# First-layer matmuls for two token blocks at once, and another order of two integer steps on GpSimd

## The chip, the cores and the metric

The kernel runs on one core of one Trainium2 chip. The metric is device time in microseconds: median of several runs. The engines are TensorE (PE, with its weight loads shown as PEld), VectorE (DVE), ScalarE (ACT), GpSimd (POOL) and SyncE (SP), which issues the DMAs.

## The reference, cut to what matters

```python
# attention, q, k, v: (8, 8, 576, 64), top_k = 32
scores = scale * np.matmul(q, k.transpose(0, 1, 3, 2))
kth = np.partition(scores, -top_k, axis=-1)[..., -top_k:-top_k + 1]
scores = np.where(scores >= kth, scores, -1000000000.0)
attn = np.exp(scores - np.max(scores, axis=-1, keepdims=True))
attn = attn / (np.sum(attn, axis=-1, keepdims=True) + 1e-09)
out = np.matmul(attn, v)
# the heads side by side: x is (4608, 512); w_in (512, 2048), w_out (2048, 512)
h = x @ w_in
g = h * (1.0 / (1.0 + np.exp(-1.702 * h)))
return g @ w_out
```

## The kernel before, in words

The attention is cut into 144 slots, 18 for each of the 8 batches. A slot is 128 rows of queries for two heads. Each batch has four full tiles of 128 tokens and a tail of 64; the tails of two batches make one block together. For a slot, TensorE computes the scores (L283), ScalarE copies them to SBUF (L295, tile `sc`), and VectorE finds the 32nd largest score of each row. From slot 12 on it does so from halves: `pair_up` takes the larger of each two scores (`greater`, VectorE, L324) and GpSimd finds the smaller (`lesser`) on the bits as integers: the sum of both (L327), less the larger (L328). Rounds of MAX8 and MATCH_REPLACE8 (L345, L348) search both halves; `pair_up` of the next slot stands in the midst of them. From the results come `cut` and, on GpSimd, `low` (L378, in slots up to 11 `cut` and `low` at L389 and L390). ScalarE masks (Prelu, L398) and takes the exponentials (L401), splits the words (L471), and a DMA through DRAM turns them. In slots up to 12, TensorE turns them instead, with a diagonal `by` (GpSimd, L414). TensorE multiplies by the values (L539, tile `o`), ScalarE copies the result (`x`, L924), and GpSimd's `x_of` scales it into the block's `xT` (L553).

When all eight heads of a block's 128 tokens are done, `finish_x` puts the block on the list `ready`. The feed-forward layers are fed to TensorE in small calls among the attention's matmuls: `hidden` does the first layer for four of a block's sixteen chunks of the hidden width (16 matmuls of 128 columns, L587, into a PSUM tile `ph`), `tanh` takes the tanh on ScalarE (L604) and copies the rest (`h`, L607), `gate` multiplies on GpSimd (L616, L617; at the end of the kernel on VectorE, L619), `project` does the second layer for the same chunks (four matmuls of 512 columns, L635, into `po`), and `leave` copies a finished `po` to `ob` (L641) and sends it out (L643). There are 36 blocks, so 144 calls of `hidden` and of `project`.

The order is written by hand and each engine works through its own queue in that order. `slot` issues slots 0 to 12, `two_slots` two slots at a time after that, with two calls of `hidden` and of `project`, and `last_slot` what is left at the end. PSUM has a pool `ps_t` with two buffers (for `o`, for every second `ph`, for transposes), `ps_h` with one (for the other `ph`) and `ps_p` with one (for `po`). The blocks' inputs `xT` come from a pool of four buffers for full tiles and one for tails, which `by` shares.

Of the kernel before, what the change touches and what calls it, by code (L numbers as in the profile page):

```python
# [9 lines left out]
ALU = mybir.AluOpType  # L10
ENG = mybir.EngineType
F32 = mybir.dt.float32
U32 = mybir.dt.uint32
I32 = mybir.dt.int32
# [4 lines left out]
P = 128  # L19
# [3 lines left out]
RAISE = 2.0**8  # L23
# [7 lines left out]
def kernel(  # L31
# [27 lines left out]
    nc = tc.nc  # L59

    B, H, S, D = q.shape
    C = H * D
    DFF = moe_w_in.shape[1]
    NP = H // 2
    NF = S // P
    FULL = NF * P
    TAIL = S - FULL
    HALF = S // 2
    CC = C // P
    FC = DFF // P  # L70
    G = 4
    NG = FC // G
# [17 lines left out]
    const = ctx.enter_context(tc.tile_pool(name="const", bufs=1))  # L90
    pool = lambda name, bufs, **kw: ctx.enter_context(tc.tile_pool(name=name, bufs=bufs, **kw))
# [6 lines left out]
    lefts = pool("lefts", 2)  # L98
    small = pool("small", 4)
    ptp = pool("ptp", 2)  # L100
    xtp = pool("xtp", 4)
    xtt = pool("xtt", 1)
    thp = pool("thp", 5)
    apart = pool("apart", 4, space=DRAM)
    apart_qk = pool("apart_qk", 2, space=DRAM)
# [1 line left out]
    ps_t = pool("ps_t", 2, space=PSUM)  # L107
    ps_h = pool("ps_h", 1, space=PSUM)
    ps_p = pool("ps_p", 1, space=PSUM)
# [4 lines left out]
    wout = const.tile([P, FC, C], F32, name="wout")  # L114
# [156 lines left out]
    st = [{} for _ in slots]  # L271
# [45 lines left out]
    greater, lesser = {}, {}  # L317

    def pair_up(n):

        sc = st[n]["sc"]
        a, b = sc[:, :, 0:HALF], sc[:, :, HALF:S]
        greater[n] = lefts.tile([P, 2, HALF], F32, name="greater", tag="left")
        nc.vector.tensor_tensor(out=greater[n][:], in0=a, in1=b, op=ALU.max)  # L324
        lesser[n] = raws.tile([P, 2, HALF], F32, name="lesser", tag="raw")
        whole = lesser[n][:].bitcast(I32)
        nc.gpsimd.tensor_tensor(out=whole, in0=a.bitcast(I32), in1=b.bitcast(I32), op=ALU.add)  # L327
        nc.gpsimd.tensor_tensor(out=whole, in0=whole, in1=greater[n][:].bitcast(I32), op=ALU.subtract)  # L328

    def topk_of_pairs(n):  # L330

# [74 lines left out]
    def divide(n):  # L406

        some = small.tile([P, 2], F32, name="some", tag="sums")
        nc.vector.tensor_scalar_add(some[:], st[n]["den"], 1e-9)
        rden = small.tile([P, 2], F32, name="rden", tag="inverse")  # L410
        nc.vector.reciprocal(rden[:], some[:])
        by = st[n]["by"] = xtt.tile([P, 2, P], F32, name="by", tag="xT_t")
        for i in range(2):
            nc.gpsimd.tensor_scalar(by[:, i, :], ident[:], rden[:, i : i + 1], 1.0, op0=ALU.mult, op1=ALU.mult)  # L414

# [62 lines left out]
        pt = st[n]["pt"] = ptp.tile([P, 2 * NF + 1, P], F32, name="pt")  # L478
        nc.sync.dma_start_transpose(out=pt[:].bitcast(U16), in_=rows[:].rearrange("q h k -> (q h) k"))

    xts = {}

    def x_at(b, t, hp):

        if t < NF:
            if (b, t) not in xts:
                xts[b, t] = xtp.tile([P, CC, P], F32, name="xT")
            return xts[b, t][:, hp, :]
        if b // 2 not in xts:
            xts[b // 2] = xtt.tile([P, CC, P], F32, name="xT_t")  # L490
        return xts[b // 2][:, hp, b % 2 * TAIL : (b % 2 + 1) * TAIL]

    def values(n, put_off=None):

# [19 lines left out]
        def bring():  # L514
            for o, hp in outs:
                to = x_at(b, t, hp)
                nc.scalar.copy(out=to, in_=o[:, 0 : to.shape[-1]])
            finish_x(n)
# [29 lines left out]
    def x_of(m, o, by):  # L548

        b, t, hps = slots[m]  # L550
        for p in range(2 if t == NF else 1):
            cols = slice(p * TAIL, (p + 1) * TAIL) if t == NF else slice(0, P)
            nc.gpsimd.tensor_tensor(out=x_at(b, t, hps[p]), in0=o[:, cols], in1=by[:, cols], op=ALU.mult)  # L553
        finish_x(m)

    def finish_x(m):

        b, t, hps = slots[m]
        if hps[-1] < NP - 1:
            return  # L560
        if t == NF:
            if b % 2:
                first = [(b - 1 + i) * S + FULL for i in range(2)]
                rows = [(slice(i * TAIL, (i + 1) * TAIL), out[x : x + TAIL, :]) for i, x in enumerate(first)]
                xT = xts.pop(b // 2)
                ready.append(([xT[:, c, :] for c in range(CC)], [rows]))
            return
        lines = out[b * S : b * S + FULL, :].rearrange("(p t) c -> p t c", t=NF)
        xT = xts.pop((b, t))
        ready.append(([xT[:, c, :] for c in range(CC)], [[(slice(0, P), lines[:, t, :])]]))  # L570

    ready = []
    hidden_at = {"f": 0}
    to_gate, gated, to_project = [], [], []
    pos = []

    def hidden(into=None):
        if not ready:
            return
        xT, rows = ready[0]  # L580
        tiles = len(rows)
        f0 = hidden_at["f"]
        fs = range(f0, f0 + G // tiles)
        ph = (into or ps_h).tile([P, G * P], F32, name="ph", tag="tp" if into else "ph")
        for i, f in enumerate(fs):
            for c in range(CC):
                nc.tensor.matmul(  # L587
                    ph[:, i * tiles * P : (i + 1) * tiles * P],
                    lhsT=win[:, c, f * P : (f + 1) * P],
                    rhs=xT[c],  # L590
                    start=(c == 0),
                    stop=(c == CC - 1),
                )
        to_gate.append((ph, fs, rows))
        hidden_at["f"] = fs.stop % FC
        if fs.stop == FC:
            ready.pop(0)

    def tanh(aside):

        if to_gate:
            ph, g, rows = to_gate.pop(0)
            th = thp.tile([P, G * P], F32, name="th")
            nc.scalar.activation(th[:], ph[:], AF.Tanh, scale=0.851 / RAISE)  # L604
            if aside:
                h = raws.tile([P, G * P], F32, name="h", tag="raw")
                nc.scalar.copy(out=h[:], in_=ph[:])  # L607
                ph = h
            gated.append((th, ph, g, rows))

    def gate(aside):
        if not gated:
            return
        th, h, g, rows = gated.pop(0)
        if aside:
            nc.gpsimd.tensor_scalar(th[:], th[:], 1.0, 1.0, op0=ALU.add, op1=ALU.mult)  # L616
            nc.gpsimd.tensor_tensor(out=th[:], in0=th[:], in1=h[:], op=ALU.mult)  # L617
        else:
            nc.vector.scalar_tensor_tensor(  # L619
                out=th[:], in0=th[:], scalar=1.0, in1=h[:], op0=ALU.add, op1=ALU.mult  # L620
            )
        to_project.append((th, g, rows))

    def project(put_off_leaving=False):

        gT, fs, rows = to_project.pop(0)
        if fs.start == 0:
            pos[:] = [
                home.tile([P, C], F32, name="po", tag=tag) for home, tag in ((ps_p, "po"), (ps_h, "ph"))[: len(rows)]
            ]  # L630
        blocks = iter(range(G))
        for f in fs:
            for po in pos:
                i = next(blocks)
                nc.tensor.matmul(  # L635
                    po[:], lhsT=gT[:, i * P : (i + 1) * P], rhs=wout[:, f, :], start=(f == 0), stop=(f == FC - 1)
                )
        if fs.stop == FC:
            def leave(po, to_rows):
                ob = thp.tile([P, C], F32, name="ob", tag="th")  # L640
                nc.scalar.mul(out=ob[:], in_=po[:], mul=0.5 / RAISE**2)  # L641
                for on, to in to_rows:
                    nc.sync.dma_start(to, ob[on, :])  # L643

            leaving.extend(lambda po=po, to=to: leave(po, to) for po, to in zip(pos, rows))
            if not put_off_leaving:
                leave_all()

    leaving = []

    def leave_all():
        while leaving:
            leaving.pop(0)()
# [16 lines left out]
    for n in by_slot:  # L670
        first = sum(map(len, list(by_slot.values())[:n]))
# [20 lines left out]
    finished = []  # L692
# [3 lines left out]

    def may_project(waiting):

        return len(to_project) > waiting and len(finished) >= NG * CC + to_project[0][1].stop

    def both_heads(to, src, t):

# [67 lines left out]
    def slot(n):  # L770
# [25 lines left out]
        for i, op in enumerate(topk_of_pairs(n) if n >= PAIRED else topk(n)):  # L796
            op()
            if i == 2:
                for _ in range(min(3 if n >= TURNS else 6, len(unfinished))):
                    finish_one()  # L800
            if i == 5:
                if n > 0:
                    divide(n - 1)
                while unfinished:
                    finish_one()
            if i == 10:
                gate(False)
# [30 lines left out]
        if n > PROJECTS and may_project(2):  # L838
            project()
        if idle:  # L840
            stay_warm(8)
        hidden()

    def last_slot():

        tanh(False)
        hidden(ps_t if hidden_at["f"] % (2 * G) else None)
        gate(False)
        if may_project(0):
            project()  # L850
# [133 lines left out]
```

## Time and profile before

| | |
|---|---|
| median of 3 runs | 1480.8 us (1480.79 to 1482.15) |
| the profiled execution's own time | 1482.51 us |
| its span | 1480.7 us |
| mean granted TensorE clock | 0.989 |
| first layer, L587 | 4608 records of 128 columns |
| second layer, L635 | 1152 records of 512 columns |
| `greater`, L324 | x132, mean 1165 ns, median 759 ns |

How to read it: busy time is the union of an engine's instructions. A matmul's record lasts longer than the array is taken by it, since matmuls overlap; what a matmul costs is seen from start to start. Each matmul of the program shows as two records. In the timeline's lines the columns are start, duration, engine, line, operation, output from input, count; brackets give the idle time before and what ended it.

### The profile page before, as it was taken

What the parts mean: (1) busy time and instruction counts of PE and PEld (TensorE: products, weight loads), DVE (VectorE), ACT (ScalarE), POOL (GpSimd) and SP (SyncE); (2) the same over time, 40 slices, a digit from 0 to 9 for tenths busy, and PEclk for the clock granted to TensorE, in tenths of its full rate; (3) what the DMA queues carried; (4) which work ended last, traced back from release to release, by engine and by line L of the source; (5) the groups of instructions that cost most, each with busy time, mean ns of one, the idle gap of its engine ahead of it and who ended that gap; (6) DMA issues with size and microseconds to landing.
All of it is one profiled execution on the core that took longest, in us unless ns stands there. A gap on an engine that the chain in (4) does not pass through costs nothing.

```text
span 1480.7 us, 31436 instructions
## 1 busy us (share of the span) xinstructions
PE 1442.7 (97%) x10784; PEld 1056.0 (71%) x10784; DVE 1382.9 (93%) x4541; ACT 1177.6 (80%) x1865; POOL 859.2 (58%) x1119
## 2 busy tenths in 40 slices
PE   7789899999999999999999999999999999999998
PEld 5667656777777777777777777777777777777776
DVE  7999989999999999999999999999999999999920
ACT  7998688878788887888878797888878798777730
POOL 3777545566655665666656556665565566665610
PEclk8899999999999999999999999999999999999999
DMA  8451256767667676776678686675767766545430
GB/s 245 135 156 51 72 159 180 202 172 179 173 181 201 159 196 179 178 189 178 170 180 200 168 193 171 183 195 163 179 175 203 174 187 184 140 131 132 127 87 15
DMA packets 516321, 242.20 MB, mean 164 GB/s; under 512 B 452672, under 2 KB 490560, under 8 KB 516160
## 3 DMA queue, kind: packets, MB, share of 16 engines
q1 hardware_dynamic: 515728, 239.89, 61.6%
q8 instruction: 85, 1.39, 0.4%
q14 instruction: 76, 0.62, 0.1%
q10 hardware_dynamic: 432, 0.30, 0.1%
HBM read 45.09 MB, written 102.24 MB: 99 GB/s over the span
## 4 chain that ended last, share of the span: by engine, by line
PE 88%; DVE 10%; ACT 2%; issue 0%; POOL 0%; POOLq 0%; ACTq 0%; DVEq 0%
PE ph L587 34%; PE po L635 32%; PE o L539 10%; PE s_ps L283 10%; DVE top L305 4%; DVE left L308 3%; PE o L528 1%; DVE top L345 1%; PE tp L449 1%; DVE wout L153 0%; DVE left L348 0%; PE none L170 0%; DVE greater L324 0%; ACT pr L401 0%; DVE win L153 0%
## 5 line engine op out<-in xcount | busy, mean ns | idle before, releaser
L635 PE MATMUL po<-wout,th 128*128 128x512 f32 x1152 | 518.6, 593 | 1.1 <-ACT ob L641 1.1
L587 PEld LDWEIGHTS ph<-xT,win 128*128 128x128 f32 x4096 | 472.1, 192 | 53.8 <-issue 52.2
L587 PE MATMUL ph<-xT,win 128*128 128x128 f32 x4096 | 484.4, 277 | 0.0
L635 PEld LDWEIGHTS po<-wout,th 128*128 128x128 f32 x1152 | 208.0, 190 | 211.0 <-issue 208.5
L345 DVE MAX8 top<-left 128x8 f32<-128x288 f32 x792 | 325.2, 445 | 0.0
L471 ACT COPY sc<-pr 128x2304 uint16<-128x2304 uint16 x132 | 278.8, 2112 | 4.2
L295 ACT ACTIVATE sc<-s_ps 128x576 f32<-128x576 f32 x288 | 170.9, 646 | 130.2 <-PE s_ps L283 130.2
L328 POOL TENSOR_TENSOR lesser<-lesser,greater 128x576 int32<-128x576 int32 x132 | 186.2, 1411 | 126.5 <-DVE greater L324 126.3
L348 DVE MATCH_REPLACE8 left<-top,left 128x288 f32<-128x288 f32 x528 | 229.6, 442 | 0.0
L401 ACT ACTIVATE pr<-sc,low 128x576 f32<-128x576 f32 x288 | 220.7, 772 | 0.0
L398 ACT ACTIVATE sc<-sc,cut 128x576 f32<-128x576 f32 x288 | 207.2, 772 | 12.4 <-DVE cut L357 5.8
L345 DVE MAX8 top<-lesser 128x8 f32<-128x288 f32 x528 | 213.5, 444 | 0.0
L327 POOL TENSOR_TENSOR lesser<-sc 128x576 int32<-128x576 int32 x132 | 187.0, 1417 | 2.4 <-ACT sc L295 2.4
L283 PE MATMUL s_ps<-qk_t 64*128 64x288 f32 (+1 forms) x1280 | 183.2, 433 | 0.3 <-ACT qk_t L219 0.3
L617 POOL TENSOR_TENSOR th<-th,h 128x512 f32<-128x512 f32 x128 | 163.7, 1279 | 10.7
L378 POOL TENSOR_SCALAR low<-cut,top 128x1 f32<-128x1 f32 x264 | 65.7, 265 | 175.6 <-DVE cut L357 174.1
L324 DVE TENSOR_TENSOR greater<-sc 128x576 f32<-128x576 f32 x132 | 153.8, 1165 | 11.7 <-ACT sc L295 5.5
L539 PE MATMUL o<-pt,v_l 128*64 128x128 f32 (+1 forms) x2368 | 144.4, 265 | 0.0
L539 PEld LDWEIGHTS o<-pt,v_l 128*64 128x64 f32 x2368 | 120.6, 138 | 25.7 <-issue 22.9
L604 ACT ACTIVATE th<-ph 128x512 f32<-128x512 f32 x144 | 85.9, 596 | 54.9 <-PE ph L587 48.3
L283 PEld LDWEIGHTS s_ps<-qk_t 64*128 64x128 f32 (+1 forms) x1280 | 99.4, 178 | 41.0 <-issue 23.1
L348 DVE MATCH_REPLACE8 left<-top,greater 128x288 f32<-128x288 f32 x264 | 114.7, 442 | 0.0
(86 smaller groups left out, 1535.7 us busy)
## 6 DMA issues: line engine op xcount, KB each, us to landing
rows<-sc SPq DMA_DIRECT2D x132, 576.0 KB, 3.2
qk_rows<-halves SPq DMA_DIRECT2D x48, 256.0 KB, 2.8
qk_l<-in_q_dram SPq DMA_DIRECT2D x64, 128.0 KB, 2.9
raw<-in_moe_w_in_dram SPq DMA_DIRECT2D x16, 512.0 KB, 4.9
v_l<-in_v_dram SPq DMA_DIRECT2D x32, 256.0 KB, 3.1
raw<-in_moe_w_out_dram SPq DMA_DIRECT2D x16, 512.0 KB, 3.5
out_dram<-ob SPq DMA_DIRECT2D x32, 256.0 KB, 2.9
qk_l<-in_k_dram SPq DMA_DIRECT2D x62, 128.0 KB, 2.9
```

What stands on the lines that cost most here:

```text
L283: nc.tensor.matmul(ps[i][rows, c, 0:HALF], lhsT=qT[b, hps[p]][on, cols], rhs=kT[b, hps[p]][on, FIRST[i] + c * HALF : FIRST[i] + (c + 1) * ...
L295: nc.scalar.mul(out=to, in_=ps[i][:, :, 0:HALF], mul=SCALE)
L327: nc.gpsimd.tensor_tensor(out=whole, in0=a.bitcast(I32), in1=b.bitcast(I32), op=ALU.add)
L328: nc.gpsimd.tensor_tensor(out=whole, in0=whole, in1=greater[n][:].bitcast(I32), op=ALU.subtract)
L345: nc.vector.max(found(r, i, True), src[:, i, :])
L348: nc.vector.match_replace(to[:, i, :], found(r, i), src[:, i, :], LOWEST)
L398: nc.scalar.activation(sc[:, i, :], sc[:, i, :], AF.Prelu, bias=cut[:, i : i + 1], alpha=HUGE)
L401: nc.scalar.activation(pr[:, i * S : (i + 1) * S], sc[:, i, :], AF.Exp, bias=low[:, i : i + 1], accum_out=den[:, i : i + 1],)
L471: nc.scalar.copy(out=halves, in_=pr[:].bitcast(U16).rearrange("p (k h) -> p h k", h=2))
L539: nc.tensor.matmul(o[j * D : (j + 1) * D, cols], lhsT=main[:, j, c, :] if c < NF else tail[:, j, :], rhs=pt[:, MAIN[j] + c if c < NF else ...
L587: nc.tensor.matmul(ph[:, i * tiles * P : (i + 1) * tiles * P], lhsT=win[:, c, f * P : (f + 1) * P], rhs=xT[c], start=(c == 0), stop=(c == ...
L635: nc.tensor.matmul(po[:], lhsT=gT[:, i * P : (i + 1) * P], rhs=wout[:, f, :], start=(f == 0), stop=(f == FC - 1))
```

## The change

`hidden` looks at the first two blocks on `ready`. If there are two, one call does two chunks for both (8 matmuls, each with 256 columns: 128 of one block and 128 of the other), else four chunks of the one as before. The chunks are taken from those that the first block still lacks, so a block's second half is computed together with its successor, which does its first half, by number, later and alone or with the block after it. All `xT` lie in one tile of five places, so that two blocks' columns can be read with one stride; `by` uses a part of place 4. Two blocks' `po` can be open at once; the second sits in `ps_h`, and `hidden` then uses `ps_t`. In `pair_up` GpSimd subtracts the larger first and adds the other score after that.

```diff
-    xtp = pool("xtp", 4)
-    xtt = pool("xtt", 1)
+    xs = const.tile([P, 5, CC, P], F32, name="xT")
...
-        nc.gpsimd.tensor_tensor(out=whole, in0=a.bitcast(I32), in1=b.bitcast(I32), op=ALU.add)
-        nc.gpsimd.tensor_tensor(out=whole, in0=whole, in1=greater[n][:].bitcast(I32), op=ALU.subtract)
+        nc.gpsimd.tensor_tensor(out=whole, in0=a.bitcast(I32), in1=greater[n][:].bitcast(I32), op=ALU.subtract)
+        nc.gpsimd.tensor_tensor(out=whole, in0=whole, in1=b.bitcast(I32), op=ALU.add)
...
-        by = st[n]["by"] = xtt.tile([P, 2, P], F32, name="by", tag="xT_t")
+        by = st[n]["by"] = xs[:, 4, 0:2, :]
...
+    class Block:
+        def __init__(self, place, rows):
+            self.place, self.rows = place, rows
+            self.left = list(range(FC))
+            self.done = 0
...
     def hidden(into=None):
         if not ready:
             return
-        xT, rows = ready[0]
-        tiles = len(rows)
-        f0 = hidden_at["f"]
-        fs = range(f0, f0 + G // tiles)
+        blocks = ready[:2]
+        many = len(blocks)
+        fs = blocks[0].left[: G // many]
+        first, step = min(x.place for x in blocks), abs(blocks[0].place - blocks[-1].place) or 1
+        blocks = sorted(blocks, key=lambda x: x.place)
+        into = ps_t if many > 1 or pos["other"] else into
         ph = (into or ps_h).tile([P, G * P], F32, name="ph", tag="tp" if into else "ph")
         for i, f in enumerate(fs):
             for c in range(CC):
                 nc.tensor.matmul(
-                    ph[:, i * tiles * P : (i + 1) * tiles * P],
+                    ph[:, i * many * P : (i + 1) * many * P],
                     lhsT=win[:, c, f * P : (f + 1) * P],
-                    rhs=xT[c],
+                    rhs=xs[:, first : first + step * (many - 1) + 1 : step, c, :],
...
+        for x in blocks:
+            x.left = [f for f in x.left if f not in fs]
+        if many > 1:
+            pos["other"] = True
+        while ready and not ready[0].left:
+            free.append(ready.pop(0).place)
+            if len(ready) < 1 or len(ready[0].left) == FC:
+                pos["other"] = False
...
     def project(put_off_leaving=False):
-        gT, fs, rows = to_project.pop(0)
...
+        gT, fs, blocks = to_project.pop(0)
+        for x in blocks:
+            if not x.done:
+                home = "ps_h" if "ps_p" in in_use else "ps_p"
+                in_use.append(home)
+                x.home = home
+                pool_of, tag = (ps_h, "ph") if home == "ps_h" else (ps_p, "po")
+                x.po = pool_of.tile([P, C], F32, name="po", tag=tag)
+        i = 0
         for f in fs:
-            for po in pos:
-                i = next(blocks)
+            for x in blocks:
                 nc.tensor.matmul(
-                    po[:], lhsT=gT[:, i * P : (i + 1) * P], rhs=wout[:, f, :], start=(f == 0), stop=(f == FC - 1)
+                    x.po[:], lhsT=gT[:, i * P : (i + 1) * P], rhs=wout[:, f, :], start=(x.done == 0), stop=(x.done == FC - 1)
                 )
...
+        for x in blocks:
+            if x.done == FC:
+                in_use.remove(x.home)
+                leaving.append(lambda x=x: leave(x))
...
     def last_slot():
 
         tanh(False)
-        hidden(ps_t if hidden_at["f"] % (2 * G) else None)
+        last["turn"] += 1
+        hidden(ps_t if last["turn"] % 2 else None)
```

More of the change, by code (lines that the diff above doesn't have):

```diff
@@ L479, in turn_by_dma @@
         nc.sync.dma_start_transpose(out=pt[:].bitcast(U16), in_=rows[:].rearrange("q h k -> (q h) k"))
-    xts = {}
+    places = {}
+    free = [4, 0, 1, 2, 3]
     def x_at(b, t, hp):
[L485 to L491, printed above, removed]
+        name = (b, t) if t < NF else b // 2
+        if name not in places:
+            at = free.pop(1 if name in ((0, 0), (0, 1), (0, 2), (0, 3)) else 0)
+            places[name] = at
+        x = xs[:, places[name], hp, :]
+        return x if t < NF else x[:, b % 2 * TAIL : (b % 2 + 1) * TAIL]
     def values(n, put_off=None):
@@ L564, in finish_x @@
                 rows = [(slice(i * TAIL, (i + 1) * TAIL), out[x : x + TAIL, :]) for i, x in enumerate(first)]
-                xT = xts.pop(b // 2)
-                ready.append(([xT[:, c, :] for c in range(CC)], [rows]))
+                ready.append(Block(places.pop(b // 2), rows))
             return
         lines = out[b * S : b * S + FULL, :].rearrange("(p t) c -> p t c", t=NF)
-        xT = xts.pop((b, t))
-        ready.append(([xT[:, c, :] for c in range(CC)], [[(slice(0, P), lines[:, t, :])]]))
+        ready.append(Block(places.pop((b, t)), [(slice(0, P), lines[:, t, :])]))
+    class Block:
[3 more added lines that the diff above has]
+            self.done = 0
+    pos = {"other": False}
     ready = []
-    hidden_at = {"f": 0}
     to_gate, gated, to_project = [], [], []
-    pos = []
     def hidden(into=None):
@@ L593, in hidden @@
                 )
[L594 to L597, printed above, removed]
+        to_gate.append((ph, fs, blocks))
+        for x in blocks:
[6 more added lines that the diff above has]
+                pos["other"] = False
     def tanh(aside):
         if to_gate:
-            ph, g, rows = to_gate.pop(0)
+            ph, g, blocks = to_gate.pop(0)
             th = thp.tile([P, G * P], F32, name="th")
@@ L608, in tanh @@
                 ph = h
-            gated.append((th, ph, g, rows))
+            gated.append((th, ph, g, blocks))
     def gate(aside):
@@ L613, in gate @@
             return
-        th, h, g, rows = gated.pop(0)
+        th, h, g, blocks = gated.pop(0)
         if aside:
@@ L621, in gate, with leave @@
             )
-        to_project.append((th, g, rows))
+        to_project.append((th, g, blocks))
     def project(put_off_leaving=False):
-        gT, fs, rows = to_project.pop(0)
[L627 to L631, printed above, removed]
+        gT, fs, blocks = to_project.pop(0)
[7 more added lines that the diff above has]
+        i = 0
         for f in fs:
-            for po in pos:
-                i = next(blocks)
+            for x in blocks:
                 nc.tensor.matmul(
-                    po[:], lhsT=gT[:, i * P : (i + 1) * P], rhs=wout[:, f, :], start=(f == 0), stop=(f == FC - 1)
+                    x.po[:], lhsT=gT[:, i * P : (i + 1) * P], rhs=wout[:, f, :], start=(x.done == 0), stop=(x.done == FC - 1)
                 )
[L638 to L647, printed above, removed]
+                x.done += 1
+                i += 1
+        def leave(x):
+            ob = thp.tile([P, C], F32, name="ob", tag="th")
+            nc.scalar.mul(out=ob[:], in_=x.po[:], mul=0.5 / RAISE**2)
+            for on, to in x.rows:
+                nc.sync.dma_start(to, ob[on, :])
+        for x in blocks:
+            if x.done == FC:
+                in_use.remove(x.home)
+                leaving.append(lambda x=x: leave(x))
+        if not put_off_leaving:
+            leave_all()
+    in_use = []
     leaving = []
@@ L697, in may_project @@
     def may_project(waiting):
-        return len(to_project) > waiting and len(finished) >= NG * CC + to_project[0][1].stop
+        return len(to_project) > waiting and len(finished) >= NG * CC + to_project[0][1][-1] + 1
     def both_heads(to, src, t):
@@ L842, in slot @@
         hidden()
+    last = {"turn": 0}
     def last_slot():
         tanh(False)
-        hidden(ps_t if hidden_at["f"] % (2 * G) else None)
+        last["turn"] += 1
+        hidden(ps_t if last["turn"] % 2 else None)
         gate(False)
```

## The prediction

> **What bounds the kernel now.** I read the page's busy shares and its chain of waits first, then busy time in stretches of 100 us, then the timeline at six places.
>
> ```profile
> span 1480.7 us, 31436 instructions
> PE 1442.7 (97%) x10784; PEld 1056.0 (71%) x10784; DVE 1382.9 (93%) x4541; ACT 1177.6 (80%) x1865; POOL 859.2 (58%) x1119
> PE 88%; DVE 10%; ACT 2%; issue 0%; POOL 0%; POOLq 0%; ACTq 0%; DVEq 0%
> ...
> 200.00:300.00 100.00, 94.51 (x643) 65.60 (x641) 98.89 (x339) 86.27 (x134) 57.32 (x77) 0.98 0.70 189
> 700.00:800.00 100.00, 100.00 (x757) 73.10 (x757) 98.48 (x336) 84.90 (x129) 60.42 (x80) 1.00 0.72 181
> ```
>
> TensorE (PE) and VectorE (DVE) both look full from 300 to 1400 us; columns two and four of the stretches are their busy times. Busy alone does not say which sets the pace. The next lines do:
>
> ```profile
> 902.45 1.41 POOL L327 TENSOR_TENSOR lesser<-sc 128x576 int32<-128x576 int32 x1
> 903.10 1.38 DVE L324 TENSOR_TENSOR greater<-sc 128x576 f32<-128x576 f32 x1
> ...
> 911.48 1.41 POOL L327 TENSOR_TENSOR lesser<-sc 128x576 int32<-128x576 int32 x1
> ...
> 913.08 0.76 DVE L324 TENSOR_TENSOR greater<-sc 128x576 f32<-128x576 f32 x1
> ...
> 1452.37 3.73 PE L587 MATMUL ph<-xT,win 128*128 128x128 f32 x32
> ...
> 1455.94 3.60 PE L635 MATMUL po<-wout,th 128*128 128x512 f32 x8
> ...
> 1459.37 3.73 PE L587 MATMUL ph<-xT,win 128*128 128x128 f32 x32
> ```
>
> The same maximum takes 0.76 us alone and 1.38 us when GpSimd's sum L327 is running. It then ends some 0.6 us after that sum ends (903.86 to 904.48), so VectorE is held by GpSimd there. That sum stands behind `x_of` (L553), which waits for TensorE's output through ScalarE's copy L924. VectorE therefore has slack, and it is stretched to TensorE's pace: both repeat every 19.11 us per pair of slots (L324 of slot 24 starts at 263.23, of slot 142 at 1390.76: 1127.5/59), and without the 0.83 us of holding in the odd slot (median 1.59 against 0.76) VectorE needs 18.28. TensorE has no gaps: starts follow starts at 3.57/32 = 111.6 ns for a first-layer record and 3.43/8 = 428.8 ns for a second-layer one, in the tail as in the middle. TensorE bounds.
>
> **The change part by part.** Every matmul of the program shows as two records (36 blocks x 16 chunks x 4 = 2304 matmuls, 4608 records). The changed kernel still makes 144 first-layer calls. In the built order of its instructions 68 of them are paired, 8 matmuls of 256 columns in place of 16 of 128: 1088 records replace 2176. The pairs lie in slots 33 to 53, 69 to 89, 105 to 125 and from 141 to the end. Elsewhere no second block is ready and nothing changes.
>
> (1) Time of a 256-column record; no row has one. From above: the line through the two rows (0.826 ns a column) gives 217.3. From below: half a 512-column record gives 214.4. I take the middle, 215.9, since the rows at both sides are the same engine and type; a pair of 128-column records takes 223.2. Saved: 7.3 ns x 1088 = 7.9 us, ends 6.4 and 9.6. The Trainium skill, "TensorE: Matmul & The Clock Gate", section "Back-to-back issue gap", speaks for less: a warm matmul costs its columns/2.4 ns plus a fixed 2.5. Taken twice per record this is 111.7 at 128 columns, as measured, but 431.7 at 512 against the 428.8 here. At 256 it gives 218.3, and 5.3 us in all. As it errs upward at 512 I keep 7.9, and 5.3 as the lower end. Worse still would be 256 columns read as two runs at 223.2: no saving (second rival). TensorE is the bound where all of these lie, so the saving counts in full.
>
> (2) GpSimd's new order. `greater` no longer meets L327, since both integer steps follow it. VectorE gains about 53 us of busy time ((1165-760) ns x 132), but becomes early, not the kernel: the next late thing for it is ScalarE's copy of scores L295, which ended 3.4 us before L324 of slot 91 and 6.8 before that of slot 92. The gain counts at 203 to 220 us, where the chain goes through VectorE. Against it: at slot 12 the first step used to run before `greater`, and now both come after it, ahead of slot 11's `cut` on GpSimd's queue.
>
> ```profile
> 144.81 0.75 DVE L324 TENSOR_TENSOR greater<-sc 128x576 f32<-128x576 f32 x1
> ...
> 145.70 1.41 POOL L328 TENSOR_TENSOR lesser<-lesser,greater 128x576 int32<-128x576 int32 x1 [4.09 <-DVE greater L324]
> ...
> 147.08 0.22 POOL L389 TENSOR_SCALAR cut<-top 128x2 f32<-128x2 f32 x1
> ...
> 147.33 1.44 ACT L398 ACTIVATE sc<-sc,cut 128x576 f32<-128x576 f32 x2 [1.97 <-POOL cut L389]
> ...
> 152.13 0.58 PE L449 MATMUL tp<-by,pr 128*128 128x128 f32 x1 [3.35 <-POOL by L414]
> ```
>
> ScalarE waits for `cut`, TensorE for `by` behind it: +1.41 us, all on the chain. At 220.14 ScalarE waited 1.00 us for VectorE's cut; VectorE saves 0.69 + 1.14 us there (slots 18 and 19), so that wait goes and gives back 1.0. Net +0.4 us, between -0.4 and +1.4.
> In every later slot the two steps take 2.82 us from 0.14 after `greater`, and `low` (L378) needs a cut that comes 2.78 after it: `low` is up to 0.25 us later. Behind it on GpSimd stand the gate L616/L617 and `x_of`. The exponentials have two Prelus of 1.44 us together ahead of them, and the gate ended at 909.79, 2.8 us before its projection at 912.63. Nothing added. With that cover gone it would be 0.25 us a slot.
>
> (3) New waits for PSUM. Paired calls take `ps_t`, so two buffers serve first call, `o` and second call. Each waits for the copy of the one two before: `x` copied at 901.54 for a call at 909.06, `h` at 907.26 for `o` at 916.07, `h` at 913.91 for a call at 921.06. Seven us or more of cover; cost nothing. But the second block's sums live in `ps_h`. Three times, at the returns from pairs to single blocks (slots 57, 93, 129), the next single first-layer call takes `ps_h` directly behind that block's last projection, and must wait for ScalarE to copy `ob` out:
>
> ```profile
> 1418.15 3.60 PE L635 MATMUL po<-wout,th 128*128 128x512 f32 x8
> ...
> 1421.59 1.61 PE L587 MATMUL ph<-xT_t,win 128*128 128x128 f32 x13
> ...
> 1421.79 0.60 ACT L641 ACTIVATE ob<-po 128x512 f32<-128x512 f32 x1 [1.97 <-PE po L635]
> ```
>
> In this place ScalarE starts 0.20 us after the projection and ends at 1422.39; with 0.06 to wake TensorE, 0.86 us each: +2.6. In the page's waits 35 of 36 `ob` found ScalarE already idle, so it should not be longer. The second layer alternates two accumulators with as many records of 428.8 ns; moving 20 `ob` copies and their output DMAs on SP's queue by one pair of slots changes no neighbour there. Nothing.
>
> (4) A pair uses a block the moment it is ready, where the older block used to go first. With scores (1.17 us) between, GpSimd's x is there in time, and a 256-column run reaches chunk c=2 after 0.86 us instead of 0.45. At slot 141 no scores are left:
>
> ```profile
> 1397.72 1.49 PE L587 MATMUL ph<-xT,win 128*128 128x128 f32 x11
> 1397.83 0.58 ACT L924 COPY x<-o 128x512 f32<-128x512 f32 x1
> ...
> 1398.50 0.60 POOL L553 TENSOR_TENSOR xT_t<-x 128x64 f32<-128x64 f32 x2 [1.65 <-ACT x L924]
> ```
>
> The pair needs the first of these products, ended near 1398.8: TensorE waits 1.1 us. At slot 145 a wait of 0.3 to 0.4 comes at c=2. +1.5 us. The common tile `xT` with five places adds no wait: a place is taken again long after its last reader.
>
> Sum on the span: -7.9 + 0.4 + 2.6 + 1.5 = -3.4 us: 1480.7 becomes 1477.3, and with the 1.8 us around the span the profiled execution's 1482.5 becomes 1479.1. The median of the runs, 1480.8, lies 1.7 below the profiled execution: 1477.4.
>
> **The rivals.** First, VectorE was the bound. Then the 63 held slots give back some 0.83 us each, 53 us, and the time is about 1430. For it: the 98.5% and the regular holding. Against it: TensorE's gapless starts, in which no VectorE gain can be spent. Chance 0.04.
> Second, slower: the array takes the two blocks, which lie apart in SBUF, as two runs of 128 columns at 111.6 ns each. Then (1) is nothing, the waits stay, and it is 1480.8 + 4.5 = 1485.3. It is slower than before as soon as a pair of records saves less than 4.5/1088 = 4.1 ns. For it: no moving operand made of two separate runs is in this trace. Against it: 512 columns take 17.6 ns less than four times 128. Chance 0.11.
> Third, pairing hardly happens: ruled out by the order (68 calls of 144), but half is what it is. Fourth, the waits of (3) and (4) are hidden after all: -7.5, 1473.3; that is inside the first case's range.
>
> **How the numbers follow.** The forecast case has 0.82, with (1) between 5.3 and 9.6 and the waits between 2.5 and 5.5: 1473.7 to 1481.0. Some 0.03 is left for a wait that I missed. About 0.2% (3.0 us) is what a measurement of this kernel can tell from no change. Within the forecast case some seven in ten gain more than that, and nearly all the rest are within it. Faster 0.60 (0.56 and 0.04), same 0.28 (0.25 and 0.03 of the second rival's milder forms), slower 0.12. Range 1473.5 to 1482.0, which adds the milder forms.
>
> **What would show it.** Records of 128x256 from ph, x1088, starting every 215.9 ns; L324's successor near 0.76 us in all slots and VectorE's idle time up by tens of us, put down to ScalarE's copy of scores; TensorE waits for `ob` three times 0.86; a later TensorE start near 153.5. It is wrong if TensorE still has no gaps but a pair takes 223 ns, if VectorE stays near 98%, or if TensorE waits recur in every pair of slots.

## The result and the profile after

| | before | changed |
|---|---|---|
| median of 20 runs each, same chips | 1482.09 us (1480.79 to 1483.96) | 1479.02 us (1477.97 to 1482.3) |
| ratio | | 0.9983, 95% interval 0.9976 to 0.9989 |
| span of the profiled execution | 1480.7 us | 1479.4 us |

By the ratio the change gains 2.5 us (1.6 to 3.6); the medians lie 3.1 us apart. The sum of the prediction was -3.4 us, from a lower median of before (1480.8, three runs).

The page of the changed kernel and its stretches of 100 us (columns two and four are TensorE's and VectorE's busy times; the one before the DMA share is the granted clock):

```profile
span 1479.4 us, 29105 instructions
PE 1436.7 (97%) x9696; PEld 1019.3 (69%) x9696; DVE 1331.9 (90%) x4541; ACT 1173.7 (79%) x1865; POOL 860.2 (58%) x1119
PE 89%; DVE 6%; ACT 3%; issue 1%; POOL 0%; POOLq 0%; DVEq 0%; ACTq 0%
...
L591 PE MATMUL ph<-xT,win 128*128 128x128 f32 (+1 forms) x3520 | 537.8, 309 | 3.4 <-ACT ob L654 2.1
...
L323 DVE TENSOR_TENSOR greater<-sc 128x576 f32<-128x576 f32 x132 | 101.0, 765 | 53.4 <-ACT sc L294 52.6
```

```profile
200.00:300.00 100.00, 95.62 (x675) 65.39 (x672) 98.93 (x352) 87.26 (x140) 59.84 (x80) 0.98 0.73 191
700.00:800.00 100.00, 100.00 (x606) 68.79 (x605) 95.36 (x340) 83.85 (x128) 61.28 (x81) 1.00 0.71 181
```

VectorE went from 1382.9 to 1331.9 us of busy time, 51 us less, and the kernel is 2.5 us faster. The maximum L323 takes 765 ns on average, as it does alone, and VectorE now stands idle ahead of it for 53.4 us, waiting for ScalarE's copy of scores. TensorE is full from 700 to 800 us as before. It has 1088 records fewer (9696 for 10784).

TensorE's timeline in the tail, where first and second layer alternate without a gap:

```profile
1437.29 3.62 PE L591 MATMUL ph<-xT,win 128*128 128x256 f32 x16
1440.74 3.60 PE L646 MATMUL po<-wout,th 128*128 128x512 f32 x8
1444.17 3.62 PE L591 MATMUL ph<-xT,win 128*128 128x256 f32 x16
```

From 1437.29 to 1440.74, 16 records of 256 columns take 3.45 us. Over the whole trace they start every 215.8 ns (forecast 215.9), 128-column ones every 111.6.

From 300 to 1390 us, three new gaps of TensorE are in the trace, all where a stretch of pairs ends. The first of them in the timeline (PE and ACT):

```profile
580.60 3.60 PE L646 MATMUL po<-wout,th 128*128 128x512 f32 x8
...
584.23 0.60 ACT L654 ACTIVATE ob<-po 128x512 f32<-128x512 f32 x1 [2.01 <-PE po L646]
...
584.88 1.38 PE L591 MATMUL ph<-xT,win 128*128 128x128 f32 x10 [0.69 <-ACT ob L654]
```

The last second-layer record starts at 583.60, and the next first-layer one 1.28 us later instead of 0.43: 0.85 us, the wait for `ob` as forecast (0.86). Near 1395 us stands the wait for the young block:

```profile
1395.79 0.59 ACT L944 COPY x<-o 128x512 f32<-128x512 f32 x1
...
1396.45 1.16 POOL L552 TENSOR_TENSOR xT<-x 128x64 f32<-128x64 f32 x4 [3.41 <-ACT x L944]
...
1396.82 3.32 PEld L591 LDWEIGHTS ph<-xT,win 128*128 128x128 f32 x16 [1.22 <-POOL xT L552]
1396.82 3.72 PE L591 MATMUL ph<-xT,win 128*128 128x256 f32 x16 [1.08 <-POOL xT L552]
```

The chain at slot 12:

```profile
145.54 0.76 DVE L323 TENSOR_TENSOR greater<-sc 128x576 f32<-128x576 f32 x1
...
146.44 1.41 POOL L326 TENSOR_TENSOR lesser<-sc,greater 128x576 int32<-128x576 int32 x1 [5.80 <-ACT raw L153]
...
147.94 1.40 POOL L327 TENSOR_TENSOR lesser<-lesser,sc 128x576 int32<-128x576 int32 x1
149.31 0.21 POOL L388 TENSOR_SCALAR cut<-top 128x2 f32<-128x2 f32 x1
...
149.55 1.44 ACT L397 ACTIVATE sc<-sc,cut 128x576 f32<-128x576 f32 x2 [3.11 <-POOL cut L388]
...
154.33 2.08 PE L448 MATMUL tp<-xT,pr 128*128 128x128 f32 x8 [4.48 <-POOL xT L413]
```

Both integer steps (L326, L327) now stand between `greater` and `cut`. `cut` starts 3.77 us after `greater` (145.54 to 149.31) against 2.27 before, and TensorE waits 4.48 us for `by` (named `xT` here, whose tile it shares) against 3.35.

To place the rest, the span is cut at the starts of the second score copies of slots 12, 14, 20, 26 and 143 in the trace. A column "12-14" is the time from slot 12's copy to slot 14's. The same cut is used for every experiment (us):

```
kernel             to slot 12   12-14   14-20   20-26   26-143   to the end
before                 137.22   20.69   60.59   56.42  1120.97   84.85
changed                137.95   23.41   60.60   55.24  1116.63   85.58
e1 pairs only          137.72   20.65   60.60   56.42  1116.63   85.58
e2 order only          135.50   23.15   60.59   55.13  1121.24   84.85
e3 longer in ps_t      137.77   23.40   60.60   55.25  1113.79   85.57
e4 slot 12 as was      137.35   21.41   60.59   53.67  1116.63   85.59
e5 e3 and e4           136.93   20.59   60.59   53.66  1113.81   85.58
e6 e5 and tail         137.10   20.66   60.59   53.66  1113.78   84.67
e7 e3, old order       137.55   20.68   60.58   56.41  1113.77   85.58
e8 changed, filled     137.33   20.58   60.59   55.29  1116.63   85.57
e9 e6, filled          135.60   19.08   60.59   55.30  1113.77   84.65
e10 before, filled     135.71   19.11   60.59   56.11  1120.97   84.84
```

The opening up to slot 12 varies by 2.5 us between single executions (135.50 to 137.95), also between kernels whose only difference lies behind it; 0.73 us of the changed kernel's span is that. The other columns repeat within some 0.1 us where nothing is changed in them, except 12-14 (20.59 to 21.41 in e4, e5 and e6, which are alike there) and 20-26, of which more below. Each row is a single execution.

### The profile page after: what moved, and what is told of

The parts are those of the page before. It is cut to its first block, busy times and chain, and to the rows that moved or that the text cites. A ratio compares the mean times of both kernels' runs of the same rounds, so it can differ in the third digit from the quotient of the medians.

```text
span 1479.4 us, 29105 instructions
## 1 busy us (share of the span) xinstructions
PE 1436.7 (97%) x9696; PEld 1019.3 (69%) x9696; DVE 1331.9 (90%) x4541; ACT 1173.7 (79%) x1865; POOL 860.2 (58%) x1119
## 3 DMA queue, kind: packets, MB, share of 16 engines
q8 instruction: 76, 1.25, 0.4%
## 4 chain that ended last, share of the span: by engine, by line
PE 89%; DVE 6%; ACT 3%; issue 1%; POOL 0%; POOLq 0%; DVEq 0%; ACTq 0%
PE ph L591 33%; PE po L646 32%; PE s_ps L282 11%; PE o L538 10%; DVE top L304 3%; DVE left L307 2%; PE tp L448 1%; PE o L527 1%; ACT pr L400 1%; ACT sc L294 0%; PE o L503 0%; ACT sc L397 0%; PE none L169 0%; DVE win L152 0%; DVE top L344 0%
## 5 line engine op out<-in xcount | busy, mean ns | idle before, releaser
L591 PEld LDWEIGHTS ph<-xT,win 128*128 128x128 f32 x3520 | 483.9, 191 | 90.1 <-issue 56.2
L591 PE MATMUL ph<-xT,win 128*128 128x128 f32 (+1 forms) x3520 | 537.8, 309 | 3.4 <-ACT ob L654 2.1
L646 PEld LDWEIGHTS po<-wout,th 128*128 128x128 f32 x1152 | 213.2, 190 | 214.5 <-issue 207.3
L552 POOL TENSOR_TENSOR xT<-x 128x128 f32<-128x128 f32 (+1 forms) x148 | 60.8, 433 | 298.0 <-ACT x L944 298.0
L326 POOL TENSOR_TENSOR lesser<-sc,greater 128x576 int32<-128x576 int32 x132 | 186.3, 1411 | 71.7 <-DVE greater L323 65.9
L327 POOL TENSOR_TENSOR lesser<-lesser,sc 128x576 int32<-128x576 int32 x132 | 186.3, 1411 | 10.4
L323 DVE TENSOR_TENSOR greater<-sc 128x576 f32<-128x576 f32 x132 | 101.0, 765 | 53.4 <-ACT sc L294 52.6
L625 POOL TENSOR_SCALAR th<-th 128x512 f32<-128x512 f32 x128 | 79.0, 617 | 120.0 <-ACT th L613 119.8
```

What stands on the lines that cost most here:

```text
L326: nc.gpsimd.tensor_tensor(out=whole, in0=a.bitcast(I32), in1=greater[n][:].bitcast(I32), op=ALU.subtract)
L327: nc.gpsimd.tensor_tensor(out=whole, in0=whole, in1=b.bitcast(I32), op=ALU.add)
L591: nc.tensor.matmul(ph[:, i * many * P : (i + 1) * many * P], lhsT=win[:, c, f * P : (f + 1) * P], rhs=xs[:, first : first + step * (many - ...
L646: nc.tensor.matmul(x.po[:], lhsT=gT[:, i * P : (i + 1) * P], rhs=wout[:, f, :], start=(x.done == 0), stop=(x.done == FC - 1))
```

## The experiments

All ratios are against the kernel before on the same chip, with 95% intervals.

**e1 and e2: each half of the change by itself.** e1 is the changed kernel with the old order:

```diff
-        nc.gpsimd.tensor_tensor(out=whole, in0=a.bitcast(I32), in1=greater[n][:].bitcast(I32), op=ALU.subtract)
-        nc.gpsimd.tensor_tensor(out=whole, in0=whole, in1=b.bitcast(I32), op=ALU.add)
+        nc.gpsimd.tensor_tensor(out=whole, in0=a.bitcast(I32), in1=b.bitcast(I32), op=ALU.add)
+        nc.gpsimd.tensor_tensor(out=whole, in0=whole, in1=greater[n][:].bitcast(I32), op=ALU.subtract)
```

> The pairing alone, with GpSimd's two integer steps in their old order (sum first). Theory A (TensorE bounds; pairing saves 7.9 us, returns to single blocks cost 2.6, late x at slots 141 and 145 costs 1.5; GpSimd's new order costs about 1.6 at the start and brings nothing later): 3.8 us faster than the kernel before, so about 1.3 faster than the changed kernel. Theory B (VectorE's relief from GpSimd is what made the changed kernel faster): no gain or a loss, 0 to 4 us slower than before. In the trace A expects the 256-column records at 216 ns, the maximum L323 again held at 1.4 to 1.9 us in every second slot, and three TensorE waits for ob.

Measured 1478.28 us, ratio 0.9975 (0.9965 to 0.9985), -3.7 us. e2 is the kernel before with the opposite edit, and no pairing.

> The kernel before with only GpSimd's two integer steps exchanged. Theory A: VectorE's maximum takes 0.76 us in all slots and VectorE loses some 50 us of busy time, but the time goes up by 0.4 to 2.8 us, from the slot where cut stands behind both steps, with TensorE still without gaps after 235 us. Theory B: some us to tens of us faster.

Measured 1482.25 us, ratio 1.0008 (0.9999 to 1.0016), +1.2 us. From the page of e2:

```profile
span 1480.5 us, 31308 instructions
PE 1442.0 (97%) x10784; PEld 1054.6 (71%) x10784; DVE 1331.4 (90%) x4541; ACT 1174.5 (79%) x1865; POOL 861.1 (58%) x1119
```

VectorE's 51.5 us less bought nothing: stretch 26-143 took 1121.24 us, 1120.97 before. TensorE's busy time is what it was. That ends the first rival, and shows that the pairing makes the gain. The times alone don't tell e2 from before, nor e1 from the changed kernel (the intervals overlap). The columns do: with the new order 12-14 is 2.46 us longer (e2 against before) or 2.76 (changed against e1), and 20-26 is 1.29 or 1.18 shorter.

**e3: the new waits for `ob` taken away.** After the last pair of a stretch, two more first-layer calls take `ps_t`:

```diff
-        into = ps_t if many > 1 or pos["other"] else into
+        into = ps_t if many > 1 or pos["other"] or pos["hold"] else into
+        pos["hold"] = max(pos["hold"] - 1, 0)
...
+                pos["hold"] = 2 if pos["other"] else pos["hold"]
                 pos["other"] = False
```

> The changed kernel, with the first-layer output kept in ps_t for two more calls after the last pair, so that no call takes ps_h while ob is still to be copied. Theory A: the three TensorE waits for ob (0.85 us each in the changed kernel's trace) are gone and nothing takes their place: 2.6 us faster than the changed kernel, 5.1 faster than before. A rival: the wait moves to another PSUM buffer, and the time stays as the changed kernel's, 2.5 faster than before.

Measured 1475.28 us, ratio 0.9963 (0.995 to 0.9975), -5.5 us. TensorE at the first return from pairs:

```profile
577.74 2.84 PE L592 MATMUL ph<-xT,win 128*128 128x128 f32 x24
580.42 3.60 PE L648 MATMUL po<-wout,th 128*128 128x512 f32 x8
583.86 2.39 PE L592 MATMUL ph<-xT,win 128*128 128x128 f32 x20
```

The first layer follows at 583.86, 3.44 us after the projection began, with no wait in brackets. 26-143 is 2.84 us shorter than in the changed kernel, and slot by slot all of it lies in three places, 0.95 to 0.96 us each (slots 58, 94, 130). That is the wait of 0.85, and 0.11 more: in the changed kernel the first record behind the wait is followed after 0.22 us (584.88 to 585.10) and not 0.11. Taking two more calls from `ps_t` makes no other wait: no new gap of TensorE is in e3's trace there.

**e4: the old order in slot 12 alone.**

```diff
+        if n == PAIRED:
+            nc.gpsimd.tensor_tensor(out=whole, in0=a.bitcast(I32), in1=b.bitcast(I32), op=ALU.add)
+            nc.gpsimd.tensor_tensor(out=whole, in0=whole, in1=greater[n][:].bitcast(I32), op=ALU.subtract)
+        else:
...
```

> The changed kernel, with the old order of the two integer steps in slot 12's pair alone. Theory A: TensorE's wait near 150 us falls from 4.5 to about 3.3 us, the half clock after it lasts one window of 3.4 us and not two, and the start is 1.5 to 2.7 us earlier: 4 to 5.2 us faster than before. A rival: the later start was jitter of the opening, and the time stays as the changed kernel's, 2.5 faster than before.

Measured 1476.68 us, ratio 0.9963 (0.9949 to 0.9976), -5.4 us. By the cut 12-14 is 2.0 us shorter than in the changed kernel and 20-26 is 1.57 shorter, though nothing is edited there. The second was unexpected; e9 bears on it. TensorE's wait for `by` fell to 3.76 us only, and one stretch of 3.4 us at half clock, as forecast, did not come. The clock of e4 (third column from the right) is at half for 6.8 us, as in the changed kernel:

```profile
150.00:152.00 2.00, 0.00 (x0) 0.00 (x0) 1.52 (x5) 2.00 (x6) 1.60 (x3) 0.63 0.00 0
152.00:154.00 2.00, 1.74 (x8) 1.75 (x9) 2.00 (x8) 0.14 (x1) 1.80 (x3) 0.50 0.02 4
154.00:156.00 2.00, 2.00 (x12) 1.78 (x11) 2.00 (x7) 0.59 (x1) 0.00 (x0) 0.50 0.00 0
156.00:158.00 2.00, 2.00 (x13) 1.21 (x12) 2.00 (x9) 0.85 (x2) 1.72 (x2) 0.66 0.00 0
```

The first 1.7 us of it fall into the wait itself, since the transposes start at 152.26. So the gain in 12-14 is the 1.47 us of the queue and a smaller part of the clock's.

**e5, e6, e7: do the terms add?** e5 joins e3 and e4.

> Both mends together: two more first-layer calls stay in ps_t after each stretch of pairs (e3), and slot 12 alone keeps the old order of GpSimd's two steps (e4). Theory A (TensorE sets the pace after 235 us, the start has a chain of its own, so terms add): the changed kernel's -2.5 us, 3 x 0.85 = 2.6 for the ob waits and 2.9 for slot 12 (e4 against the changed kernel) give about -8 us against before, ratio 0.9946; no start of a TensorE record comes 1.28 us after the one before it at a change from L646 to L591, and one of 1.3 us is left near 1390. Theory B (something else, VectorE or a DMA, is the floor some 5 us below before): no better than either alone, -5.5 us, and new TensorE gaps appear in the place of those taken away.

Measured 1473.97 us, ratio 0.9942 (0.993 to 0.9955), -8.6 us. The terms add (-8 was forecast); no floor appears. e6 adds to it that the second call at slot 141 takes the older block alone:

```diff
                 ready.append(Block(places.pop(b // 2), rows))
+                pos["alone"] = b == B - 1
...
-        blocks = ready[:2]
+        blocks = ready[:1] if pos["alone"] else ready[:2]
+        pos["alone"] = False
```

> e5, and at slot 141 the second first-layer call uses the older block alone (four of its chunks) in place of a pair with the block whose x has only just been started. Theory A: the gap of 1.3 us near 1390 goes (1.1 us of waiting), two calls fewer are paired, 32 records of 215.8 ns again as 64 of 111.6 (0.2 us more): about -9 us against before, 0.9 below e5. Theory B (the block's x is late for the next call too, or the wait turns up at slot 143 or 145): the time of e5, and a gap of about 1 us at another place after 1390.

Measured 1472.90 us, ratio 0.9937 (0.9924 to 0.9951), -9.3 us. The intervals of e5 and e6 overlap, so the times alone don't part them; the cut does: only the last column differs, 84.67 against 85.58, 0.91 less as forecast. In TensorE's timeline of e6 the calls stand end to end there:

```profile
1387.62 3.84 PE L598 MATMUL ph<-xT,win 128*128 128x128 f32 x32
1391.30 3.60 PE L654 MATMUL po<-wout,th 128*128 128x512 f32 x8
1394.73 1.46 PE L598 MATMUL ph<-xT,win 128*128 128x256 f32 x6
```

e7 is e3 with the old order (e1's edit) in every slot.

> The pairing with e3's longer stay in ps_t, and the old order of GpSimd's steps in every slot. Theory A (the new order pays only at 203 to 220 us, where the chain goes through VectorE, and costs only at slot 12): e1's -3.7 us and 2.6 for the ob waits give -6.3 us against before, that is 1 to 2.7 us slower than e5, and the difference to e5 has all arisen by slot 22. Theory B (VectorE's relief is of use through the whole kernel once TensorE is faster): it falls behind e5 slot by slot and ends near -4 us, with TensorE gaps that end on VectorE.

Measured 1476.36 us, ratio 0.9959 (0.9946 to 0.9971), -6.1 us. It is behind e5 by 2.75 us in 20-26 and nowhere else from slot 12 on (26-143 is 1113.77 against 1113.81). Some 1.6 of that is a stretch at half clock which e7 has there and e5 lacks (see e9); the rest is the shorter gap of the new order. So even with a faster TensorE the new order is of use in those six slots and in no other.

**e8: is the clock the missing term?** From 12 to 14 the changed kernel lost 2.72 us, of which the order of GpSimd's queue explains 1.41 as forecast. The granted clock of before (first fence) and of the changed kernel (second; clock in the third column from the right):

```profile
150.00:152.00 2.00, 0.00 (x0) 0.00 (x0) 1.65 (x6) 2.00 (x6) 1.60 (x3) 1.00 0.00 0
152.00:154.00 2.00, 1.87 (x9) 1.88 (x10) 2.00 (x6) 0.00 (x1) 2.00 (x4) 0.53 0.01 4
154.00:156.00 2.00, 2.00 (x13) 1.80 (x12) 2.00 (x7) 0.76 (x2) 1.03 (x1) 0.61 0.00 0
156.00:158.00 2.00, 2.00 (x26) 1.43 (x24) 2.00 (x8) 1.22 (x4) 1.40 (x1) 1.00 0.00 0
```

```profile
152.00:154.00 2.00, 0.00 (x0) 0.00 (x0) 1.42 (x4) 2.00 (x6) 1.60 (x3) 0.91 0.00 0
154.00:156.00 2.00, 1.67 (x8) 1.67 (x9) 2.00 (x8) 0.23 (x1) 1.88 (x3) 0.50 0.02 4
156.00:158.00 2.00, 2.00 (x10) 1.82 (x9) 2.00 (x6) 0.59 (x1) 0.00 (x0) 0.50 0.00 0
158.00:160.00 2.00, 2.00 (x11) 1.35 (x12) 2.00 (x9) 0.85 (x2) 1.64 (x2) 0.50 0.00 0
160.00:162.00 2.00, 2.00 (x26) 1.25 (x23) 1.93 (x9) 1.19 (x2) 1.65 (x3) 0.88 0.00 0
```

Before works at half clock for some 3.4 us after its gap, the changed kernel for some 6.8. e8 fills the gap, directly ahead of the transposes that wait for `by`, with matmuls whose sums are never read:

```diff
+        if n == PAIRED:
+            none = ps_t.tile([P, 512], F32, name="tp")
+            for i in range(18):
+                nc.tensor.matmul(none[:, 0:P], lhsT=ident[:], rhs=ident[:], start=True, stop=True)
         if n >= TURNS:
             turn_main(n - 1)
```

> The changed kernel with 18 matmuls of 128 columns on constant data added to TensorE's queue in slot 12, directly ahead of the transposes that wait for by; their sums are never read. They fill about 4.0 of the 4.75 us in which TensorE had nothing. Theory C (the part of the loss that was not forecast comes from the clock that an idle TensorE is granted afterwards): the granted clock stays near 1.00 from 148 to 162 us, where the changed kernel had 0.5 for 6.8 us; the scores' copies of slots 14 and 15 come 1.2 us or more earlier than in the changed kernel against slot 12's; 1 to 3 us off the time at the end. Theory D (the 1.2 us came from an order of queues behind cut and by, the clock being only a sign of idleness): the copies of slots 12 to 14 lie as in the changed kernel, and the time is the same within 0.5 us.

Measured 1476.56 us, ratio 0.9963 (0.9951 to 0.9976), -5.5 us. TensorE's timeline and the clock of e8:

```profile
148.32 4.18 PE L834 MATMUL tp<-ident 128*128 128x128 f32 x36
153.74 2.05 PE L448 MATMUL tp<-xT,pr 128*128 128x128 f32 x16 [1.24 <-POOL xT L413]
```

```profile
154.00:156.00 2.00, 2.00 (x20) 1.80 (x19) 2.00 (x7) 0.75 (x2) 1.29 (x2) 1.00 0.02 4
156.00:158.00 2.00, 2.00 (x26) 1.42 (x24) 2.00 (x6) 1.22 (x4) 0.31 (x1) 1.00 0.00 0
158.00:160.00 2.00, 2.00 (x16) 1.11 (x13) 1.97 (x8) 0.56 (x2) 1.92 (x2) 1.00 0.00 0
```

The transposes still wait for `by` and begin 16.4 us after slot 12's copy, as in the changed kernel, so no queue has moved. But then they run at full clock: 16 records of L448 in 2.05 us, where the changed kernel did 8 in 2.08. 12-14 falls from 23.41 to 20.58, and all other columns from slot 12 on stay. So 2.83 us of 12-14 are the clock's, and theory D is out.

**e9, e10: the same on the best version and on before.** e9 is e6 and e10 the kernel before, each with the filling of e8 but fewer matmuls, since the gap is shorter with the old order:

```diff
-            for i in range(18):
+            for i in range(14):
```

> All three mends of e6 (two more calls in ps_t after each stretch of pairs, the old order of GpSimd's steps in slot 12, the older block alone at slot 141) and 14 matmuls on constant data (3.1 us, sums never read) in TensorE's gap at slot 12. Theory C (a gap of 3.5 us still buys a stretch at half clock, which the matmuls prevent): clock 1.00 from 148 to 162 us and 1.0 to 1.7 us less than e6, so about -10.7 us against before, ratio 0.9928. Theory D (after the old order is back there, the chain through VectorE at 203 to 220 us takes up what slot 12 saves): the time of e6, with the same clock of 1.00.

> The kernel before with the 14 matmuls on constant data in TensorE's gap at slot 12, nothing else. Theory C: its one stretch at half clock (0.53 and 0.61 from 152 to 156 us) becomes 1.00, the scores' copies from slot 14 on come some 1.5 us earlier against slot 12's than in before, and 0.5 to 1.5 us is gained at the end (part of it may be given back by slot 22, where the chain goes through VectorE). Theory D (half clock over transposes that wait for others anyway costs nothing): slots 12 to 14 as in before, and the same time within 0.5 us.

e9: 1472.14 us, ratio 0.9933 (0.992 to 0.9947), not told apart from e6. e10: 1481.52 us, ratio 0.9993 (0.9984 to 1.0002), no measurable gain where 0.5 to 1.5 was forecast. In both, 12-14 is some 1.58 us shorter than without filling, as theory C said: the price of one stretch at half clock there. In e9, however, 20-26 is 1.64 us longer than in e6. The clock of e6, and then of e9, in that stretch:

```profile
220.00:224.00 4.00, 2.66 (x13) 1.41 (x11) 3.97 (x17) 3.97 (x7) 0.40 (x1) 1.00 0.54 114
224.00:228.00 4.00, 3.25 (x37) 2.44 (x39) 3.93 (x14) 2.62 (x8) 3.30 (x4) 1.00 0.80 188
228.00:232.00 4.00, 4.00 (x45) 3.35 (x40) 4.00 (x18) 3.97 (x8) 0.87 (x2) 1.00 0.64 185
```

```profile
220.00:224.00 4.00, 2.31 (x11) 1.43 (x11) 3.97 (x13) 2.25 (x6) 2.37 (x2) 0.81 0.94 212
224.00:228.00 4.00, 4.00 (x48) 3.30 (x46) 3.97 (x16) 2.91 (x5) 0.92 (x3) 0.76 0.50 109
```

Both have the same gap of TensorE shortly before (2.13 us from one start to the next, at 222.38 and 219.31). e6 keeps full clock after it, e9 gets half clock for some 3.4 us. The same split holds in every trace with this gap: e4, e5 and e6 at 1.00 (20-26 in 53.66 to 53.67), the changed kernel, e2, e3, e8 and e9 at half (55.13 to 55.30). Theory D had the time right for e9 and the reason wrong: not VectorE's chain took the gain up, but another stretch at half clock.

## Why the prediction was right, and which term was mis-sized

The forecast 1477.4 was 1.6 below the median of 1479.0; 1.3 of that is the base (1482.1 here against 1480.8). The change of -3.4 lies inside the measured -1.6 to -3.6. The range of 1473.5 to 1482.0 nearly reaches the old time, so that the median fell into it says little; the terms say more. The prediction also took 3.0 us as the least that can be told from no change and gave more than that the larger chance. By the ratio the gain is smaller, and twenty runs of each kernel tell it from nothing all the same. (The fourth rival's 1473.3 was called inside the first case's range; it lies 0.4 below it.) By its steps, from slot 12 on, in the profiled execution:

- (1), the 256-column record: right. 215.8 ns for 215.9, so each saves 7.4 against two of 128. In 26-143 lie 60 of the 68 paired calls: 60 x 16 x 7.4 = 7.1 us. In e3, where the waits are gone, that stretch is 7.18 shorter than before. The formula of the Trainium skill ("TensorE: Matmul & The Clock Gate", "Back-to-back issue gap"), taken twice per record, gave an estimate of 218.3 ns, or 960 x 4.9 = 4.7 us here; the measurement decides against it. The second rival (two runs of 128) fell by the same number.
- (3), the three waits for `ob`: right, 0.85 us each for the 0.86 forecast, with 0.11 more each for the slower start behind them, and no other wait for PSUM. 26-143 was to be 4.4 shorter (7.0 saved, 2.6 waited) and is 4.34.
- (4), the late x: right at slot 141 (1.08 us in brackets), and at slot 145 the record that starts at 1430.62 is held 0.32 us longer than the others (0.3 to 0.4 forecast). The last stretch was to be 0.6 longer (1.5 less the 0.9 of eight paired calls) and is 0.73.
- (2), GpSimd's order: the step that was mis-sized, +0.4 forecast and +1.54 measured (+2.72 in 12-14, -1.18 in 20-26). "+1.41 us, all on the chain" priced the queue alone. With the clock at 1.00 on both sides (e8 and e10), the order costs 20.58 - 19.11 = 1.47, so that part was right. The other 1.25 is the clock: half clock costs 23.41 - 20.58 = 2.83 in the changed kernel and 20.69 - 19.11 = 1.58 before. The prediction priced what TensorE waits and not the clock it wakes to, though the rows of 2 us show it in the kernel before (0.53 and 0.61). The give-back was -1.18 for -1.0.
- The claim that TensorE bounds, and that 53 us of VectorE's time buys nothing beyond slot 26, held: e2 there is no faster than before.

The cost of the clock follows the time at half clock in which the transposes and what is behind them run. It is 3.2 to 3.4 us in before, e1, e5, e6 and e7, and 12-14 is 1.5 to 1.6 us longer there than with filling and the same order. It is 5.1 us in e4 (2.3 longer), 5.6 in e2 (2.6 longer), 6.1 in the changed kernel and e3 (2.8 longer).

Together (2) and the others make -2.05 from slot 12 on, and 0.73 of varying opening makes the span's -1.3. The medians differ by more than this one pair of traces. The runs' own clocks suggest why: of the 20 runs of the changed kernel, the 8 with a mean clock of 0.986 or 0.987 took 1479.1 to 1482.3 us, and the 12 with 0.988 to 0.990 took 1478.0 to 1480.7. The profiled execution is of the first group. Whether it is the stretch at slot 12 or another that parts them stays open.

The version with all mends, e6, is 1472.9 us, 6.8 us faster than the changed kernel by the two ratios; the filling of e9 adds nothing that can be measured.

## What to carry to other kernels

An engine that is 98% busy is not the bound if its instructions stretch to another's pace: look for the one whose starts have no gaps, and test by relieving the other alone. When an edit lengthens a gap of TensorE, read the clock behind the gap, in rows of 2 us, and price it with the wait. A pairing that saves nanoseconds per record must be checked for the places where it returns to single work: the buffer that the second block borrowed is handed back there, and moving two calls to another pool gave back 2.8 us.

## What the runs showed of the hardware

The clock after a gap is a step, not a slope: at slot 12 it stood at 0.5 for 3.4 us or for 6.8 us, and cost this kernel 1.5 to 1.6 us or 2.3 to 2.8 us. The gap's length alone does not set which. Gaps of 3.4 to 3.9 us (start to start; before, e1, e5, e6, e7) brought 3.4 us, gaps of 4.75 us (changed, e2, e3) brought 6.8, and so did e4's of 4.04. The gap of 2.13 us in 20-26 brought half clock in five traces and none in three.

What else sets it can be read from the clock records of the twelve traces. In each trace all stretches at half clock start on one grid of 3.413 us, within 3 ns, whatever the gaps did, and where the grid lies differs between executions. In e5 and e6 a line of the grid falls into the gap of 2.13 us, and the clock stays full. In the five that dropped the whole gap lies between two lines, with 1.31 to 1.53 us of TensorE's busy time beside it. In e4 it does too, with 1.56 us, and the clock stayed full: that is the edge. The Trainium skill ("TensorE: Matmul & The Clock Gate", Part 1) describes an activity window of some 3.4 us that runs freely. The grid agrees with that. The section also says that the drop comes after at least one idle window; here it came after steps of the grid in which TensorE was busy for more than a third of the time, and the measurement decides.

So an edit ahead of such a gap moves it against the grid, and a gain of a microsecond there is uncertain: between e6 and e9, 20-26 changed by 1.64 us though nothing in it was edited. As the grid also differs between executions, the 20-26 column of a single trace (53.66 or 55.2) need not be that of the kernel's other runs.

A moving operand of two runs of 128 columns that lie apart in SBUF took 215.8 ns a record. That is what a contiguous one would take by interpolation (an estimate of 214.4 to 217.3 from the records of 128 and 512 columns); a contiguous one was not run.
